# Moving one rest projection out of the last segment into the feed-forward network, with new load and copy orders and a new list of planner biases

## The chip, the cores and the metric

The kernel runs on one core of one Trainium2 chip. The metric is device time in microseconds (us), the median of several executions. A core has five instruction streams that run beside each other and meet at semaphores: TensorE (PE, with its weight loads listed as PEld), VectorE (DVE), ScalarE (ACT), GpSimd (POOL) and SyncE (SP). SP issues most DMAs; ACT issues a few at the start.

## The reference

What is computed is one transformer layer over 2048 tokens of width 640. The attention half is recurrent: the tokens come in 64 segments of 32, each segment puts 8 memory rows in front of its 32 tokens, attends within these 40 rows with 32 heads of 128, and hands the first 8 rows of its output to the next segment as memory.

```python
for s in range(n_seg):                       # 64 segments
    xs = x[:, s*32:(s+1)*32, :]              # of layernorm(x)
    h = concatenate([mem, xs], axis=1)       # 8 + 32 rows
    q, k, v = (einsum('btd,dhe->bhte', h, W) for W in (Wq, Wk, Wv))
    scores = where(mask, einsum('bhqe,bhke->bhqk', q, k) * scale, -1e9)
    o = einsum('bhqk,bhke->bhqe', softmax(scores), v)
    o = einsum('bhte,hed->btd', o, Wo)
    mem = o[:, :8, :]
    outs.append(o[:, 8:, :])
h = x + concatenate(outs)
hn = layernorm(h)
gate, up = hn @ W_gate, hn @ W_up            # width 1728
out = h + (gate * (gate > 0) * up) @ W_down
```

## The kernel before, in words

**Main rows and rest rows.** Of the 40 rows of a segment, 32 (8 of memory and the first 24 tokens) are the main rows, and the last 8 tokens are the rest rows. Nothing later in the recurrence needs the rest rows' output. So the queries, keys and values of the rest rows of four segments (a "quad") are computed together, in six parts (function `rest`: two query, two key and two value groups), and the output projection of the rest rows of eight segments together (`rest_o`, eight pieces of 16 matmuls, then a copy into `osr`, and `rest_out` stores it to DRAM). `oTr` keeps the rest rows' attention output until then. Five quads' rest parts are computed while the weights still load (`EARLY = 5`); the others are spread over the segments as filler for PE.

**A segment** (`segment`, called 64 times): queries, keys and values of the main rows (`groups`, line 1561), scores (lines 1860 and 1864), exponentials, sums, and the product with the values (1899, 1904), then the output projection in two halves: `wo_early` (1932) goes to a bank of its own and is kept as a high and a low part in `half`, `wo` (1951) goes to the bank BW, `wo_add` (1968) adds the two parts there. From BW the new memory rows are copied into the input of the next segment (1673) and transposed (1676), which the next segment's first matmul needs; BW is also evicted to `osb` and stored. `load_rs` brings the rest rows' queries, keys and values of the next segment from DRAM into `RS`. For the first segment they come straight from SBUF instead: POOL copies queries and keys (line 1596, the four "RS0" copies), and eight small DMAs on ACT's queue bring the values (line 1605).

**The feed-forward network** (`ffn`, four blocks of 512 tokens): 27 groups of five matmuls for gate and up (1729), the ReLU on ACT (1746), the product on DVE into `gT` (1748), and the projection down (1762, and 1539 for its last 128 columns). Its weights overwrite the attention weights: `Wg`, `Wu` and `Wl` go where Wq was, `Wd` and the second block's tokens `xn2T[1]` where Wk was. Three empty POOL instructions (named B0, B1, B2) wait for the last readers of Wq, Wk and Wv. The second halves of `Wg` and `Wu`, and `Wd` and `Wl`, also wait for `("osb", 1)`, that is for the last segment's eviction. `ln2` prepares 128 tokens of input (the last two are named tn2) with 20 PE transposes (1703).

**What sets the order.** Every instruction is described by `op` with what it reads and writes, a duration, and for a DMA a latency `lat` and a transfer time `xfer`. A list scheduler (`_Sched.schedule`) plays these through in simulated time and always takes the ready instruction of the highest level; the level is the length of the chain behind it plus entries of a dictionary `BIAS`, per name or per name and segment. `ENGINE` does the same for the choice between ACT and DVE. The result is one fixed order for each engine. In `op`, `x=` uses a buffer in sequence, and `beside=` reads it beside other readers: an instruction with `beside` waits for the last `x` user of that buffer, and if that is a DMA, for its landing.

Of the kernel before, what the change touches and what calls it, by code (L numbers as in the profile page):

```python
# [101 lines left out]
    "QK0mm@52": 27.88, "QK0mm@53": -4.68, "QK1mm@53": 4.98, "ln2l@62": 13.26, "sc1@62": -3.61,  # L102
    "ln2hd@62": 10.81, "Q1mm@62": -6.46, "Q0mm@64": 8.09, "QTx@64": -2.17, "QTx@63": -8.42, "exp1@62": -2.42,
    "mask0@63": 8.07, "sum0@64": -12.03, "QTx@51": -3.23, "oTev1@62": -0.16, "sum0@62": 1.43,
    "woadd@63": -14.73, "Q0mm@63": 5.22, "K1mm@64": -4.8, "ln1@64": -1.18, "hiev@64": -0.37, "loev@64": -6.44,
    "r0T@13": -7.71, "r0T@23": -0.83, "ln2s0@24": -1.25, "r0T@28": -0.32, "r1T@15": -7.85, "r0T@15": 39.2,
    "ln2s1@20": 18.36, "r1T@24": 6.73, "r0T@30": 7.0, "r0T@41": 9.76, "r0T@2": -4.21, "r0T@8": 4.31,
    "r1T@10": 8.26, "r1T@21": -1.66, "r0T@34": -44.8, "r1T@35": -14.61, "r0T@35": 5.08, "r0T@46": 7.34,
    "r1T@50": 20.94, "er1T@0": 6.64, "er0T@0": -26.24, "r1T@3": 22.75, "r1T@5": -2.15, "r1T@8": -22.29,
    "r0T@9": 20.78, "r1T@14": -3.91, "r0T@18": 3.15, "ln2a@24": 13.36, "r0T@25": 9.56, "r1T@36": 0.02,  # L110
    "r0T@39": 1.08, "r1T@40": 11.66, "r0T@44": -2.9, "r1T@45": 3.51, "r1T@47": 3.89, "r0T@49": -0.32,
    "r0T@51": 2.95, "r1T@52": 0.76, "r1T@55": -2.63, "r0T@55": -3.49, "r0T@56": 3.81, "r1T@57": 6.98,
    "ln2n@62": -3.77, "mask1@63": 0.92, "sum1@63": 7.18, "K0ev@62": -9.88, "mem1@63": -6.51, "loev@63": 2.39,
    "V1ev@63": 6.09, "K1ev@63": 0.32, "V0ev@64": 0.58, "rec1@64": -6.08, "K0Tev@64": -5.8, "K1ev@64": -10.81,
    "V1mm@64": -0.18, "oTev0@64": 2.09, "Q0Tev@64": -1.41, "wo1@64": 6.66, "Q0ev@64": 0.81, "sum1@64": -12.04,
    "mul0@64": -2.8, "K0ev@64": -11.69, "relu@65": 25.24, "tn2s0@65": -1.18, "Q1ev@64": -10.94,
    "tn2nd@65": -3.0, "hld@65": 17.53, "outdma@65": 9.49, "ordma@64": -2.27, "exp0@64": 8.26, "mask0@64": -8.5,
    "Q1mm@64": -7.79, "tn2go@65": -4.67, "tn2hd@65": 2.15, "V0mm@64": -4.09, "xnld@65": 3.31, "tn2x@65": 8.72,
    "tn2s1@65": 0.3, "ln0@64": 0.66, "pv0@64": 8.76, "tn2lx@65": -0.14, "tn2a@65": 5.97, "hadd@65": -8.82,
    "tn2lo@65": 18.63, "tn2Tev@65": 66.88, "gmul@65": 38.27, "mask1@64": -2.1, "ordma@61": 0.68,  # L120
    "K1mm@62": -2.64, "ln2a@32": 1.68, "mem1@54": 19.25, "ln2s0@20": 4.7, "ln2lx@32": 1.54, "ln2T@40": 0.7,
    "QTx@54": -1.51, "mask0@60": 19.52, "mask0@62": -1.74, "mask0@61": -3.7, "rec1@62": 4.5,
    "mask1@62": -25.63, "memcp0@61": -5.77, "ln2x@40": 4.41, "mask1@57": -2.39, "V1ev@57": -4.21,
    "rsdma@59": -7.2, "mask1@59": -16.78, "ln2s0@30": 8.32, "ln2lo@32": 7.27, "ln2l@32": 22.24,
    "ln2s1@54": -2.75, "wo1@54": -23.1, "mem1@56": -5.5, "mask0@57": 17.55, "ln2lx@20": 1.69, "ln2hd@24": -6.4,
    "ln2x@32": -1.4, "ln2l@24": 1.61, "ln2h@24": 2.68, "ln2s0@32": -11.95, "ln2h@32": 1.55, "ln2hd@32": 16.71,
    "rsdma@36": -0.43, "ln2a@38": -32.25, "QTx@31": 16.39, "ln2h@20": -1.42, "ln2s1@24": -5.03,
    "ln2lx@38": 0.61, "rsdma@8": 1.0, "ln2s0@38": 8.48, "ln2T@24": -19.85, "QTx@28": 0.22, "ln2a@30": -0.12,
    "rsdma@4": -14.78, "rsdma@29": 0.41, "rsdma@7": -13.97, "ln2n@24": -3.43, "rsdma@21": 4.61,
    "rsdma@26": 0.46, "ln0@44": -19.76, "ln2T@48": 7.82, "QTx@25": 0.35, "ln2Tev@32": -3.04, "QTx@36": 6.15,  # L130
    "ln2T@38": -9.4, "mask0@49": -23.75, "memcp0@50": -4.66, "mask0@51": 1.55, "QTx@3": 1.1, "QTx@8": 5.1,
    "oTev0@11": 9.98, "ln2n@20": -14.18, "ln2l@20": 0.52, "ln2a@22": 0.34, "QTx@6": -9.67, "mask1@14": -4.57,
    "rsdma@15": 0.65, "mask0@15": -5.34, "rsdma@16": 10.8, "mask1@18": 12.67, "ordma@21": -11.36,
    "ln2h@22": 4.04, "ln2go@22": 6.72, "mem1@22": -8.44, "mul1@32": 16.46, "mask1@32": -7.94, "mask0@32": 8.03,
    "QTx@35": -0.91, "QTx@41": -5.6, "rsdma@42": -28.29, "rsdma@44": -6.1, "QTx@45": 10.15, "ln2h@46": -4.12,
    "mask1@45": -34.49, "mask1@8": 0.75, "mask1@9": -9.21, "Q0ev@9": 4.52, "mask1@10": 20.02, "mul0@11": -6.33,
    "mask0@11": -0.34, "QTx@12": -5.38, "mask1@11": -6.32, "rsdma@12": 21.59, "mask1@13": -12.11,
    "QTx@17": 0.18, "QTx@20": -1.41, "ln2s1@22": -22.73, "rsdma@23": -3.62, "ln2Tev@24": 4.24,
    "rec0@25": 11.71, "mask1@25": -10.43, "mask1@26": -4.35, "mask0@26": 11.01, "rsdma@28": -9.74,
    "oTev1@27": -3.41, "ln2s1@30": 5.57, "rsdma@30": 2.9, "ln2go@30": 13.11, "mask0@29": -2.33,  # L140
    "mul0@32": -13.05, "osbev@32": -11.15, "rsdma@34": -7.0, "r0mm@34": 3.46, "mask1@36": -1.19,
    "mask0@36": -6.31, "ln2s1@38": -2.92, "ln1a@37": 5.12, "rvev@38": -7.09, "K0Tev@38": -3.05,
    "K1ev@38": 4.09, "ln0@38": 25.33, "mask1@40": -21.13, "ln1@39": -12.34, "ln2nd@40": 1.61, "oTr@40": 1.21,
    "V1mm@40": -23.61, "pv1@42": 15.48, "wo0@41": -12.36, "mask1@44": 2.73, "QTx@47": -7.4, "mask1@47": 0.39,
    "wo1@48": -6.53, "woadd@48": -0.94, "Q1Tev@48": -22.44, "rec0@49": 14.97, "K1ev@50": -22.66,
    "mask1@52": 2.07, "rsdma@56": 23.48, "mask1@56": -13.76, "mask0@55": 6.73, "mem@57": 3.55, "pv0@56": 37.91,
    "K0mm@57": -1.0, "K1mm@57": -7.64, "ln1@57": 0.04, "QTx@58": -0.49, "oTr@57": 1.27, "Q0Tev@57": -0.75,
    "mask0@58": 5.69, "ln1st@57": 22.78, "K0ev@57": -7.75, "QTx@59": -6.65, "mask1@58": -4.84,
    "memcp1@59": -23.71, "mask1@60": -4.13, "rsdma@60": -7.28, "mask0@3": 0.21, "rsdma@5": -0.43,
    "mask0@4": 0.63, "mask0@9": -1.77, "rsdma@11": 1.74, "mask0@12": -0.31, "K0ev@13": -8.19,  # L150
    "mask0@16": -1.48, "rec0@20": -12.18, "mul0@20": 8.24, "ln2s0@22": 4.2, "ln2hd@22": -8.09,
    "mask0@22": -6.66, "rec0@22": 5.09, "mask1@24": 14.94, "K1ev@24": 5.7, "mask0@25": 13.6, "mask1@27": 4.96,
    "mem@27": 1.4, "mask0@27": 2.3, "loev@27": -2.04, "ln1x@29": 6.46, "mask0@28": 4.98, "V0mm@28": -0.14,
    "Q0ev@28": 0.07, "mask0@30": 1.91, "mask0@33": 17.07, "exp0@33": -17.09, "Q0ev@34": 7.51, "mask0@34": 0.01,
    "mask1@34": 11.47, "rsdma@35": 15.6, "mask1@35": 11.79, "mask0@35": -48.34, "pv1@36": -13.73,
    "sum0@37": -34.01, "ln1st@37": -0.63, "rec1@37": -27.48, "ln2nd@38": 7.35, "wo1@37": -6.45,
    "mask0@38": -0.44, "ord@40": 3.35, "mask0@39": 0.2, "mask0@40": 70.66, "Q0ev@40": 12.0, "ln1a@41": -33.12,
    "mask0@41": -17.95, "mask1@41": -0.08, "mask0@43": -27.08, "rvev@42": 8.57, "mask0@42": -9.38,
    "woadd@42": -4.45, "mul1@42": 2.47, "mask1@42": -0.36, "memcp1@42": -21.72, "rec0@42": -5.61,
    "ln1@45": -4.83, "mask0@45": 13.85, "QTx@46": -1.55, "mul1@46": 0.02, "ln2go@46": -0.06, "ln1a@45": -8.84,  # L160
    "ln2Tev@46": -4.54, "loev@46": -3.2, "mask1@46": -7.16, "mask0@47": 3.07, "mask0@48": 16.0,
    "Q0ev@48": 8.46, "mask1@48": -3.59, "odma@48": -3.95, "oTev0@48": -1.77, "wo0@48": 4.31, "mem1@49": 5.25,
    "mask1@49": 2.88, "K0ev@49": 7.94, "mask1@50": 7.95, "mask0@52": 7.12, "mask0@53": 0.32, "mask1@53": 1.8,
    "mask1@54": 3.2, "ln2hd@54": -17.49, "mask0@54": 7.2, "odma@56": -23.33, "mask1@55": -21.92,
    "ln1@56": 4.16, "woadd@56": -0.17, "mem1@3": 0.36, "oTr@5": 0.37, "mask0@6": 20.33, "K1mm@8": -0.72,
    "mask0@8": -39.65, "ln1@10": 11.1, "sum1@10": -19.62, "mask0@10": -10.12, "mem@12": 2.29, "mask1@12": 0.3,
    "mask0@13": -2.1, "mask1@15": 5.83, "mask1@16": -0.88, "odma@16": 33.32, "rsdma@17": -4.35,
    "ln1n@17": -4.15, "memcp1@18": -7.07, "rsdma@18": -0.42, "K0mm@17": 28.43, "ro@17": 15.04,
# [1093 lines left out]
def build_kernel(nc, A_x, A_mem0, A_Wq, A_Wk, A_Wv, A_Wo, A_seg_len, B_x, B_W_gate, B_W_up,  # L1262
# [816 lines left out]
    for k in normed + list(range(NQ - 2, NQ)):  # L2079
        ln2(k)  # L2080
# [66 lines left out]
```

## Time and profile before

| | |
|---|---|
| median of 3 runs | 1050.86 us (1050.62 to 1051.02) |
| the profiled execution, its own time | 1052.89 us |
| its span, first to last instruction | 1051.2 us |
| PE busy | 993.4 us (95%) |
| DVE, ACT, POOL busy | 652.5, 488.1, 108.4 us |
| span 0 to 74 us (weights load) | PE busy 51.66 us |
| span 74 to 860 us (segments 2 to 64) | PE busy 756.28 us |
| span 896 to 1051.2 us (most of the feed-forward network) | PE busy 151.89 us of 155.20 |

The profiled execution is 1.69 us longer than its span and 2.03 us longer than the median of the runs. PE counts as busy while a matmul streams, whatever the clock; the granted clock is a column of its own in the table by stretches. In a row of the timeline the columns are start, length, engine, line, operation and tiles, then in brackets the idle time of the engine before it and what ended it. "issue" means that the engine waited for nothing that the profile shows.

### The profile page before, as it was taken

How to read it: one execution, taken by the hardware profiler on the slowest of the kernel's cores; microseconds unless marked ns; L12 is line 12 of the kernel's file. 1: busy time of each engine (PE TensorE's matmuls, PEld its weight loads, DVE VectorE, ACT ScalarE, POOL GpSimd, SP SyncE). 2: the span in 40 equal slices, each digit the busy share in tenths (PEclk: the TensorE clock that was granted, in tenths of full speed). 3: DMA queues.
4: the chain of work that ended last, by engine and by line, in shares of the span. 5: the costliest groups of instructions: out<-in, count | busy, mean ns of one | idle time of the engine just before them, and what ended most of it. 6: DMA issues, size and time to landing. Idle time of an engine off the chain costs nothing.

```text
span 1051.2 us, 53190 instructions
## 1 busy us (share of the span) xinstructions
PE 993.4 (95%) x24820; PEld 534.8 (51%) x23828; DVE 652.5 (62%) x1404; ACT 488.1 (46%) x1161; POOL 108.4 (10%) x262
## 2 busy tenths in 40 slices
PE   5699999999999999999999999999999989999998
PEld 2245555655565555655555555655555444444443
DVE  4457767677777767776777677667865642432233
ACT  2334555455556545555665455645554632121210
POOL 2301101011011101110101011011110010000000
PEclk9999999999999999999999999999999999999999
DMA  9991112121222112221222122212211237111101
GB/s 328 397 286 47 49 37 55 32 54 50 80 54 73 38 42 60 73 66 33 80 69 54 32 69 58 66 28 76 70 49 31 77 117 219 65 38 44 32 20 57
DMA packets 119212, 84.26 MB, mean 80 GB/s; under 512 B 71556, under 2 KB 115148, under 8 KB 118988
## 3 DMA queue, kind: packets, MB, share of 16 engines
q1 hardware_dynamic: 115628, 78.13, 24.9%
q8 instruction: 191, 3.13, 1.3%
q10 hardware_dynamic: 3360, 2.73, 0.8%
q14 instruction: 33, 0.27, 0.1%
HBM read 55.05 MB, written 25.69 MB: 77 GB/s over the span
## 4 chain that ended last, share of the span: by engine, by line
PE 86%; DVE 4%; ACT 2%; issue 2%; DMA 1%; ACTq 0%; POOL 0%; SPq 0%
PE ps L1561 45%; PE ps L1729 11%; PE ps L1932 7%; PE ps L1951 7%; PE ps L1762 5%; PE ps L1647 3%; PE ps L1899 2%; PE ps L1539 2%; PE ps L1874 1%; PE ps L1860 1%; DVE xT L1676 1%; DVE xm L1673 1%; DVE oT L1402 1%; DMA RS<-stg 1%; ACTq L1605 0%
## 5 line engine op out<-in xcount | busy, mean ns | idle before, releaser
L1401 ACT ACTIVATE tok<-ps 128x512 bf16<-128x512 f32 x241 | 142.2, 596 | 177.6 <-PE ps L1561 162.5
L1561 PE MATMUL ps<-Wk,xT 128*32 128x512 bf16 x2560 | 178.0, 380 | 14.2 <-DVE xT L1676 10.2
L1561 PE MATMUL ps<-Wq,xT 128*32 128x512 bf16 x2560 | 178.4, 379 | 6.1 <-DVE xT L1676 6.0
L1561 PE MATMUL ps<-Wv,xT 128*32 128x512 bf16 x2560 | 175.2, 380 | 0.2 <-DMA Wv<-in_A_Wv_dram 0.2
L1981 DVE STREAM_TRANSPOSE KT<-tok 128x512 bf16<-128x512 bf16 x128 | 89.6, 704 | 35.2 <-ACT tok L1401 33.7
L1981 DVE STREAM_TRANSPOSE QT<-tok 128x512 bf16<-128x512 bf16 x128 | 90.3, 706 | 32.8 <-ACT tok L1401 30.1
L1561 PEld LDWEIGHTS ps<-Wk,xT 128*32 128x32 bf16 x2560 | 67.1, 96 | 82.3 <-DVE xT L1676 20.9
L1561 PEld LDWEIGHTS ps<-Wq,xT 128*32 128x32 bf16 x2560 | 67.5, 96 | 72.2 <-DVE xT L1676 12.2
L1402 DVE CAST oT<-ps 128x320 bf16<-128x320 f32 x127 | 60.3, 488 | 54.7 <-PE ps L1904 51.8
L1932 PE MATMUL ps<-Wo,oT 128*32 128x320 bf16 x2048 | 90.9, 300 | 3.3 <-DVE oT L1402 3.2
L1951 PE MATMUL ps<-Wo,oT 128*32 128x160 bf16 x4096 | 86.2, 233 | 6.6 <-issue 4.9
L1746 ACT ACTIVATE g<-ps 128x512 bf16<-128x512 f32 (+1 forms) x56 | 33.4, 596 | 124.8 <-PE ps L1729 124.8
L1951 PEld LDWEIGHTS ps<-Wo,oT 128*32 128x32 bf16 x4096 | 74.3, 97 | 22.2 <-DVE oT L1402 9.5
L1748 DVE TENSOR_TENSOR gT<-g,ps 128x512 bf16<-128x512 bf16 (+1 forms) x56 | 37.5, 686 | 77.3 <-PE ps L1729 47.1
L1401 ACT ACTIVATE oT<-ps 128x320 bf16<-128x320 f32 x129 | 54.0, 435 | 54.9 <-PE ps L1904 53.2
L1561 PEld LDWEIGHTS ps<-Wv,xT 128*32 128x32 bf16 x2560 | 59.7, 96 | 38.0 <-ACT tok L1401 1.0
L1846 POOL COPY QT<-RS 128x256 bf16<-128x256 bf16 x64 | 25.8, 403 | 457.6 <-PE ps L1864 457.1
L1402 DVE CAST tok<-ps 128x512 bf16<-128x512 f32 x79 | 52.9, 670 | 24.8 <-PE ps L1561 24.5
L1869 ACT ACTIVATE E<-ps 128x224 bf16<-128x224 f32 x128 | 45.6, 356 | 43.0 <-PE ps L1864 42.2
L1729 PE MATMUL ps<-xn2T,Wg 128*128 128x512 bf16 x260 | 63.3, 379 | 0.3 <-DVE gT L1748 0.3
L1729 PE MATMUL ps<-xn2T,Wu 128*128 128x512 bf16 x260 | 63.3, 379 | 0.0
L1762 PE MATMUL ps<-Wd,gT 128*128 128x512 bf16 x224 | 61.7, 379 | 0.0
(93 smaller groups left out, 1444.6 us busy)
## 6 DMA issues: line engine op xcount, KB each, us to landing
RS<-scr_qk SPq DMA_DIRECT2D x63, 128.0 KB, 2.3
big<-in_A_x_dram SPq DMA_DIRECT2D x36, 160.0 KB, 2.8
scr_qk<-stg SPq DMA_DIRECT2D x44, 128.0 KB, 2.2
Wq<-in_A_Wq_dram SPq DMA_DIRECT2D x10, 512.0 KB, 7.3
Wk<-in_A_Wk_dram SPq DMA_DIRECT2D x10, 512.0 KB, 7.4
Wv<-in_A_Wv_dram SPq DMA_DIRECT2D x10, 512.0 KB, 8.1
Wo<-in_A_Wo_dram SPq DMA_DIRECT2D x8, 640.0 KB, 10.8
scr_v<-stg SPq DMA_DIRECT2D x32, 128.0 KB, 2.7
```

Of the source, the lines that this page charges most:

```text
L1401: return e.activation(dst, src, ACTF.Copy)
L1402: return e.tensor_copy(dst, src)
L1561: o = pe.matmul(out, lhs[c], rhs, start=(c == 0), stop=(c == DC - 1), skip_group_check=True)
L1647: o = pe.matmul(bank(bk)[p0:p0 + 32, 0:2 * SLICE], oTr[b][:, 16 * g + 4 * j + i, 32 * y:32 * y + 32], cols(h, 2 * a, 2 * a + 2), start=(h ...
L1729: o = pe.matmul(bank(bk)[:, 0:TB], lhs(c), xT[:, :, c * 128:(c + 1) * 128], start=(c == 0), stop=(c == DC - 1))
L1746: op("act", lambda a, t=t, lo=lo, hi=hi, bg=bg: a.activation(g1[t.at][lo:128, :], bank(bg)[0:hi, 0:TB], ACTF.Relu), r=["B2"], x=[bg, t], d ...
L1748: op("dve", lambda v, t=t, lo=lo, j=j, bu=bu: v.tensor_tensor(gT[lo:128, j, :], g1[t.at][lo:128, :], bank(bu)[lo:128, 0:TB], ALU.mult), r= ...
L1762: pe.matmul(bank(ba)[:, 0:512], lhs, Wd[:, j, 0:512], start=(j == 0), stop=(j == FC - 1), skip_group_check=True)
L1869: op("act", lambda a: a.activation(E[:, g, :, 0:56], sco(BS[g]), ACTF.Exp, scale=SCALE), r=["table"], w=[("E", g)], x=[BS[g]], dur=0.36, n ...
L1932: o = pe.matmul(bank(BA)[p0:p0 + 32, 0:2 * SLICE], oT[:, 4 * jj + i, XR:40], cols(h, 2 * b2, 2 * b2 + 2), start=(i == 0 and jj < 2), stop= ...
L1951: o = pe.matmul(bank(BW)[32 * j:32 * j + 32, 0:SLICE], oT[:, 16 + 4 * jj + i, XR:40], cols(h, j, j + 1), start=(i == 0 and jj == 0), stop= ...
L1981: op("dve", lambda v, tb=tb, dst=dst: v.transpose(dst, tok[tb.at][:, :].rearrange("p (h r) -> p h r", r=32)), w=[("QT" if p == 0 else "KT" ...
```

## The change

It does five things.

1. The last eight segments' `rest_o` no longer stands in segment 64. It is called after `ffn(0)`, in four parts of two pieces each, and part k waits for the product `gT[2k+1]` of the first block. The last two `ln2` and blocks 1 to 3 follow in the program's text; the scheduler decides the order of instructions as before.
2. The second block's tokens (`xnld` of block 1) wait for the load of `Wl`, the last of the feed-forward weights. Before, they waited for B1 alone.
3. The four RS0 copies stand ahead of the stores of the same buffers and no longer wait for these stores to land. The stores read the buffer beside them.
4. Three figures of the planner change: 1.09 for 0.8 us (the POOL copy `ord`), 3.4 for 2.0 us (latency of the eight value DMAs), and 1.0 us more for the first weight load.
5. `BIAS` is another list (2142 entries with another value, 591 new, 481 gone, spread over all segments), and so is `ENGINE` (71 changed, 159 new, 128 gone).

```diff
@@ rest / spread
-                    stg[t1.at]...(u i k)...), x=[t1, t2], dur=0.8, name=early + "ord")
-            op("act" if early else "sp", lambda e: e.dma_start(
-                scr_qk[q, 2 * p + g, :, :], stg[t2.at][:, :]), w=[("scr_qk", q, p, g)], x=[t2], dur=0.4,
-               lat=2.2, chan=("rqe", 12) if early else ("rq", 4), name=early + "rdma", xfer=0.35)
+                    stg[t1.at]...(u i k)...), x=[t1, t2], dur=1.09, name=early + "ord")
             if q == 0:
                 k = 2 * p + g
                 op("pool", lambda e: e.tensor_copy(RS[0][:, 128 * k:128 * k + 128], stg[t2.at][:, 0:128]),
                    w=[("RS0", k)], beside=[t2], dur=0.31, name="RS0")
+            op("act" if early else "sp", lambda e: e.dma_start(
+                scr_qk[q, 2 * p + g, :, :], stg[t2.at][:, :]), w=[("scr_qk", q, p, g)], beside=[t2], dur=0.4,
+               lat=2.2, chan=("rqe", 12) if early else ("rq", 4), name=early + "rdma", xfer=0.35)
@@ rest / values
-                       w=[("RSv0", g, j)], beside=[tb], dur=0.7, lat=2.0, chan=("rv0", 8), name="ldrs", xfer=0.05, desc=2)
+                       w=[("RSv0", g, j)], beside=[tb], dur=0.7, lat=3.4, chan=("rv0", 8), name="ldrs", xfer=0.05, desc=2)
@@ ffn
-            op("sp", ... scr_n[4 * b + u]), r=[("scr_n", 4 * b + u)] + (["B1"] if home else []),
+            op("sp", ... scr_n[4 * b + u]), r=[("scr_n", 4 * b + u)] + (["B1"] if home else []) + ["Wl"] * (b == 1),
@@ load_w
-           xfer=xfer + (1.4 if nload[0] == 2 else 0.0), desc=desc)
+           xfer=xfer + {1: 1.0, 2: 1.4}.get(nload[0], 0.0), desc=desc)
@@ segment
-        if s == NSEG - 1:
-            rest_o(s // 8, B("rest"), (0, 8))
-            rest_out(s // 8)
@@ behind the loads of the feed-forward weights
+    ffn(0)
+    bk = B("rest")
+    for k in range(4):
+        rest_o(NSEG // 8 - 1, bk, (2 * k, 2 * k + 2), [("gT", 2 * k + 1)])
+    rest_out(NSEG // 8 - 1)
     for k in normed + list(range(NQ - 2, NQ)):
         ln2(k)
-    for b in range(NBLK):
+    for b in range(1, NBLK):
         ffn(b)
```

## The prediction

> **What bounds the kernel now.** I read the page first, then the chain of work that ended last, then three places where it leaves PE's matmuls: the end of the segments, the start, the gaps between segments.
>
> ```profile
> PE 993.4 (95%) x24820; PEld 534.8 (51%) x23828; DVE 652.5 (62%) x1404; ACT 488.1 (46%) x1161; POOL 108.4 (10%) x262
> ...
> PE 86%; DVE 4%; ACT 2%; issue 2%; DMA 1%; ACTq 0%; POOL 0%; SPq 0%
> ```
>
> PE bounds it: 95% busy and 86% of the chain. The change takes no matmul away, so it can only win time in which PE idles or runs at a lower clock, and lose by adding such time.
>
> The end of the segments, PE's timeline, then the table by stretches (length, busy times by engine, then granted clock, DMA share, GB/s):
>
> ```profile
> 859.00 0.74 PE L1951 MATMUL ps<-Wo,oT 128*32 128x160 bf16 x32 [0.66 <-DVE oT L1402]
> 859.55 0.86 PE L1647 MATMUL ps<-Wo,oTr 128*32 128x320 bf16 x18
> 862.53 5.54 PE L1647 MATMUL ps<-Wo,oTr 128*32 128x320 bf16 x110 [2.13 <-issue]
> ...
> 868.70 2.33 PE L1729 MATMUL ps<-xn2T,Wg 128*128 128x512 bf16 x10
> ```
>
> ```profile
> 862.00:864.00 2.00, 1.47 (x24) 0.95 (x28) 0.00 (x0) 0.00 (x0) 0.00 (x0) 0.58 0.44 167
> 864.00:866.00 2.00, 2.00 (x40) 1.22 (x33) 0.00 (x0) 0.00 (x0) 0.00 (x0) 0.56 0.05 15
> ```
>
> The 128 matmuls to be moved (L1647) stand ahead of the second half of the last segment's projection. After 18 of them PE idles 2.13 us for "issue", and then runs at a clock of 0.56 until 866. The page lists 191 packets in its instruction queue q8; 24820 + 23828 PE instructions over 191 are 255 each: a packet is a page of PE's instructions. The trace has such packets at 851.27 and 860.09 us, 8.8 us apart where four or five is usual, while the feed-forward weights load. I read the 2.13 us as a late page.
>
> SP's timeline over the same time:
>
> ```profile
> 852.64 1.75 SPq L1722 DMA_DIRECT2D xn2T<-scr_n  x4
> 854.43 0.43 SPq L2069 DMA_DIRECT2D Wg<-in_B_W_gate_dram  x1
> 854.90 0.53 SPq L2069 DMA_DIRECT2D Wu<-in_B_W_up_dram  x1
> 869.15 0.37 SPq L2069 DMA_DIRECT2D Wg<-in_B_W_gate_dram  x1
> ```
>
> The first weights land 7.4 and 9.9 us after issue, at 861.8 and 864.8. The second halves go out at 869.15 only, behind the last eviction.
>
> **The tail, step by step.** Matmuls of L1647 at full clock come at 1.09 us per 32 elsewhere in the chain, so 128 are 4.36 us wherever they stand. From 859.73 to 868.76 there are 9.03 us: 4.36 for them, about 0.8 for the rest of L1951 and the adding, and 3.8 of loss (2.13 idle, 1.7 at the low clock: 5.47 us for the 110 against 3.75).
>
> After the change PE goes from 859.73 straight to the adding and is ready for the feed-forward network at 860.5. SP need not issue four token loads first: Wg goes out when Wq's last reader (853.7) is through, at 854.0 to 854.4, and 640 KB less stand before it. The second halves, alone on the queues, landed 5.1 us (960 KB) and 7.8 us (both) after the first issue; scaled to 1120 KB that is 6.0 and 9.1, hence Wg at 860.2 and Wu at 863.3. Two gate groups (2 x 1.08) bridge from 860.5 to 862.7, so about 0.5 us of waiting is left. The 3.8 us of loss go, if no page is late.
>
> What is added: four visits of L1647 between wide matmuls. The nearest rows are the transposes inside the network:
>
> ```profile
> 898.09 1.24 PE L1729 MATMUL ps<-xn2T,Wg 128*128 128x512 bf16 x5
> 899.26 0.46 PE L1703 MATMUL ps<-ident,big 128*32 128x128 bf16 x20
> 899.65 1.25 PE L1729 MATMUL ps<-xn2T,Wu 128*128 128x512 bf16 x5
> ```
>
> Five wide matmuls take 1.08 us start to start, here 1.17 and (to the next transposes, at 900.84) 1.19: 0.10 us for a change of tile shape, eight changes 0.8 us (bounds 0, if the visits go side by side, and 1.2). Tail: 3.8 - 0.5 - 0.8 = **2.5 us won**. Bounds: 3.3 won; 0.8 lost, if idle time and low clock return.
>
> The rest of the tail costs nothing. The second weight halves go out some 8 us earlier. Block 1's tokens go behind Wl: landed at about 884 before (877.89 + 6.5), plus 1.75 us of issue and 2.6 to land is 888.5, and block 1's first group runs at about 902 (25 of the 160 gate and up matmuls before 907.8 are its own). SP waits in order, and behind these four loads stand the `osr` stores, the last two `ln2` and the loads of scr_h; a few us there are covered, since the last two `ln2` feed only block 3, after 990. That cover gone, it would be 1 us for 1 us.
>
> **The start.** PE's longest wait from 46 to 74 us (total, times, longest), and POOL's timeline:
>
> ```profile
> PE ps L1860 <- POOL QT L1846: 2.5, 1, 2.5
> ```
>
> ```profile
> 46.38 0.29 POOL L1596 COPY RS<-stg 128x128 bf16<-128x128 bf16 x1 [0.24 <-DMA scr_qk<-stg]
> ...
> 48.98 0.29 POOL L1596 COPY RS<-stg 128x128 bf16<-128x128 bf16 x1
> 49.45 0.40 POOL L1846 COPY QT<-RS 128x256 bf16<-128x256 bf16 x1 [0.17 <-POOLq L1837]
> ```
>
> The first scores wait for L1846, which waits for the RS0 copies, which wait for stores to land and stand behind further copies. Ahead of the stores the last RS0 copy can run at about 43.3, where its source is done. The idle 2.52 us at 47.4 then need not be; nor the low clock behind it (0.5 from 49.96 to 56.79; 48 wide matmuls there cost 2.6 us more). But PE lacks weights: the last four loads of Wv land at 48.2, 50.2, 51.8 and 53.4 (issue plus 8.8 to 9.2), so much of that idle time only moves. The end of this stage is floored too: the last Wo load goes out at 58.1 and lands 10.6 later, at 68.7; a quarter of L1951 (0.28), the adding (0.3), copy and transpose (about 1.3) let segment 2 start at 70.6 against 73.84. So 0 to 3.2 us; I take **1.3 won**, below the middle, because the eight value DMAs still issue one by one behind Wv (57.10 to 62.87, the last lands at 67.92).
>
> **The segments.** From segment 2 to 64 PE idles 28.6 us in gaps of over 0.15 us; the largest causes from 74 to 856:
>
> ```profile
> PE ps L1561 <- DVE xT L1676: 16.2, 35, 0.8
> PE ps L1951 <- issue: 4.9, 11, 1.0
> ```
>
> The new biases redo the order in every segment. Bounds: all new gaps and all old ones are the same kind, so half of the 16.2 us lost or won. Nothing in the profile says which; I take **0**, with 3 us either way.
>
> **The sum.** 1052.89 - 2.5 - 1.3 = 1049.1 for the profiled execution. It stands 2.03 above the median, so **1047.0 us**, 0.37% faster.
>
> **Rivals.**
> - *The tail wait stays* (0.25). A late page needs the weights' traffic and some 250 quick PE instructions; both remain up to 860.5, and then the network issues 10 per 1.08 us, which any page survives. In my count the page ends 36 instructions after 859.73, still inside L1951; some 40 instructions fewer ahead of it and it falls into the network. If it stays, so does the low clock: 0.8 lost, 1.3 won, 1050.4. The Trainium skill ("TensorE: Matmul & The Clock Gate", Part 1) lets the clock halve only after an idle window of about 3.4 us; by that rule the same wait would leave the clock full and this rival would give 1048.7. The trace speaks against it: 0.56 after 2.13 us.
> - *The segments win more* (0.15): a quarter of their idle time less 3 us already in the range, so 4 us beyond the sum: 1043.
> - *Slower* (0.10): late pages inside the segments. Eleven waits of L1951 for "issue" cost 4.9 us now, 0.45 each. A tighter order sends the narrow matmuls in denser runs; if their number doubles, the tail's wait stays and the start gives nothing, it is 1050.9 + 4.9 + 0.8 = 1056.6. With these two it decides from three more such waits. Against it: at 0.4 us idle per segment there is little room to be denser.
> - *It does not do what it says*: the scheduler could put the four parts together after block 0's last gate group. That saves six shape changes, 0.6 us, and stays within the forecast.
>
> Of the page wait itself the Trainium skill ("Runtime: NRT & Kernel Launch", Instruction fetch mechanics) says that PE holds 2048 instructions and that a refill is mostly hidden; by it no page could be late here and the tail's 2.5 us would be safe. The 2.13 us beside the packet at 860.09 say otherwise.
>
> **Chances.** Forecast 0.50, within about 2 us of 1047.0. What a measurement of this kernel can tell from no change is about 0.2%, 2.1 us: faster means below 1048.8. Of the forecast 0.42 lies there, of the stayed wait 0.05, of the third case all 0.15: faster 0.62; same 0.28; slower 0.10. The range is 1043.0 to 1051.0: it leaves out the slower rival and a little of the segments' win.
>
> **What would show it.** Right: no L1647 before the first L1729 of the network, that one at 860 to 862, no "issue" of over 1 us and a clock of 1.0 from 858 to 870; L1846's first run at 44 to 47; segment 2 (its first L1561 on xT) at 71 to 73. Wrong: an "issue" wait before the network, or a wait of the network for Wu of over 1 us; PE's idle time in the segments up by over 3 us; block 1 waiting for its tokens.

## The result: 0.56% slower

The changed kernel takes 1055.83 us in the median (1053.47 to 1058.48) beside 1050.63 us (1048.27 to 1054.4) for the kernel before in the same comparison: a ratio of 1.0056, 95% interval 1.0038 to 1.0074. The prediction, 1047.0 us within 1043.0 to 1051.0, was wrong, in sign too. Below, each experiment stands against runs of the kernel before taken beside it. Single executions of one kernel spread over up to 10.6 us, so a verdict rests on ratios of medians, and the place of a gain or loss on the stages of one profiled execution, which lies between 3.2 us below the median of its kernel and 2.8 above: a difference of a few us between whole spans, or in the long stretch of segments 2 to 60, can be the choice of execution.

The profiled execution after takes 1058.48 us, the slowest of its seven; its span is 1056.4 us, 5.2 more than before. The page of the kernel after, its engines and its chain:

```profile
PE 997.4 (94%) x24804; PEld 535.4 (51%) x23828; DVE 668.1 (63%) x1429; ACT 475.3 (45%) x1136; POOL 109.4 (10%) x262
...
PE 86%; DVE 4%; DMA 2%; issue 2%; ACT 1%; SPq 0%; ACTq 0%; DVEq 0%
```

PE still bounds it, and a DMA has come into the chain. I cut the span where DVE starts to copy the new memory rows (L1673 before, L1702 after), once per segment:

| us | start, to segment 2 | segments 2 to 60 | 61 | 62, 63 | 64 to the end | span |
|---|---|---|---|---|---|---|
| before | 72.85 | 739.22 | 12.67 | 23.81 | 202.62 | 1051.2 |
| after | 78.36 | 734.54 | 15.14 | 23.51 | 204.87 | 1056.4 |
| difference | +5.51 | -4.68 | +2.47 | -0.30 | +2.25 | +5.2 |

Three places lose and one wins.

**The start.** PE's timeline after, then three of the waits from 46 to 74 us (total, times, longest):

```profile
63.78 1.47 PE L1590 MATMUL ps<-Wv,xr 128*32 128x512 bf16 x24
70.07 0.32 PE L1928 MATMUL ps<-E,Vm 32*128 32x40 bf16 x16 [4.82 <-DVE stg L1431]
```

```profile
ACT stg L1430 <- DMA scr_qk<-stg: 7.0, 2, 4.7
DVE stg L1431 <- DMA scr_qk<-stg: 6.2, 2, 4.2
...
PE ps L1889 <- POOL QT L1875: 2.6, 1, 2.6
```

PE idles 4.82 us for copies into `stg`, and both copying engines wait for stores of scr_qk to land. Behind the wait the granted clock is low, the last column but two here:

```profile
69.20:76.00 6.80, 5.67 (x120) 3.23 (x124) 3.23 (x6) 2.19 (x5) 0.00 (x0) 0.50 0.76 171
```

The line of L1889 above is the wait that was to go; before it was 2.5. ACT's timeline over the same time, and the time from issue to landing in the table of DMAs from 56 to 72 us:

```profile
56.07 6.20 ACTq L1634 DMA_DIRECT2D RS<-stg  x8
62.31 0.95 ACTq L1624 DMA_DIRECT2D scr_qk<-stg  x2
...
70.05 0.60 ACT L1430 ACTIVATE stg<-ps 128x512 bf16<-128x512 f32 x1 [4.74 <-DMA scr_qk<-stg]
```

```profile
scr_qk<-stg ACTq DMA_DIRECT2D x2, 128.0 KB, 7.0
```

Two early stores stand on ACT's queue behind the eight value DMAs, go out at 62.31 and need 7.0 us beside the last loads of Wo. The planner has given two of the six value copies behind them the same two staging buffers (numbers 4 and 5; in the kernel before, the three behind the stores took 9 to 11), reckoning with 2.95 us for such a store. POOL's timeline shows why the wait for QT stayed:

```profile
43.21 5.57 POOL L1617 COPY stg<-stg 128x512 bf16<-128x512 bf16 x5 [0.86 <-DMA scr_qk<-stg]
48.95 0.40 POOL L1875 COPY QT<-RS 128x256 bf16<-128x256 bf16 x1 [0.17 <-POOLq L1866]
```

The last RS0 copy ended at 42.35, sooner than predicted. But the copy of the queries, L1875 (L1846 before), stands behind five `ord` copies in the new order, and runs at 48.95 where it ran at 49.45.

**The end of the segments.** PE's timeline after, SP's, and one stretch (length, busy times by engine, then the clock):

```profile
861.90 1.01 PE L1980 MATMUL ps<-Wo,oT 128*32 128x160 bf16 x47 [0.66 <-DVE oT L1431]
865.43 0.83 PE L1980 MATMUL ps<-Wo,oT 128*32 128x160 bf16 x17 [2.53 <-issue]
...
866.46 4.45 PE L1758 MATMUL ps<-xn2T,Wg 128*128 128x512 bf16 x10
870.70 2.62 PE L1758 MATMUL ps<-xn2T,Wu 128*128 128x512 bf16 x10
```

```profile
857.02 0.38 SPq L2095 DMA_DIRECT2D Wg<-in_B_W_gate_dram  x1
857.44 0.53 SPq L2095 DMA_DIRECT2D Wu<-in_B_W_up_dram  x1
```

```profile
866.00:868.00 2.00, 2.00 (x20) 0.65 (x6) 0.32 (x1) 0.00 (x0) 0.00 (x0) 0.50 0.10 15
```

The rest projection is gone from here, yet the wait for "issue" is there, 2.53 us now, in the next instructions that came: the second half of the last segment's projection. The half clock behind it now covers the network's first ten matmuls, 4.24 us instead of 2.16.

**The segments.** From 74 to 812 us the two largest waits of PE, before and then after:

```profile
PE ps L1561 <- DVE xT L1676: 14.1, 31, 0.8
PE ps L1951 <- issue: 4.9, 11, 1.0
```

```profile
PE ps L1590 <- DVE xT L1705: 13.1, 30, 0.7
PE ps L1980 <- issue: 3.6, 9, 0.8
```

Segment 61 gives half of the gain back; PE's timeline, then SP's:

```profile
822.37 0.28 PE L1928 MATMUL ps<-E,Vm 32*128 32x40 bf16 x16 [1.38 <-DMA RS<-scr_v]
```

```profile
814.19 0.56 SPq L1637 DMA_DIRECT2D scr_v<-stg  x1
...
817.87 1.14 SPq L1657 DMA_DIRECT2D RS<-scr_v  x2
```

The last quad's values are stored at 814.19 and read back from 817.87 on; PE waits 1.38 us for them, and a stretch of half clock (3.41 us from 823.5) follows.

### The profile page after: what moved, and what is told of

Read it like the earlier page. It is cut to its first block, busy times and chain, and to the rows that moved or that the text cites. A ratio compares the mean times of both kernels' runs of the same rounds, so it can differ in the third digit from the quotient of the medians.

```text
span 1056.4 us, 53183 instructions
## 1 busy us (share of the span) xinstructions
PE 997.4 (94%) x24804; PEld 535.4 (51%) x23828; DVE 668.1 (63%) x1429; ACT 475.3 (45%) x1136; POOL 109.4 (10%) x262
## 4 chain that ended last, share of the span: by engine, by line
PE 86%; DVE 4%; DMA 2%; issue 2%; ACT 1%; SPq 0%; ACTq 0%; DVEq 0%
PE ps L1590 44%; PE ps L1758 11%; PE ps L1961 7%; PE ps L1980 7%; PE ps L1791 4%; PE ps L1676 3%; PE ps L1928 3%; PE ps L1568 2%; PE ps L1903 1%; DMA scr_qk<-stg 1%; PE ps L1889 1%; DVE xT L1705 1%; DVE xm L1702 1%; PE ps L1933 0%; DVE oT L1431 0%
## 5 line engine op out<-in xcount | busy, mean ns | idle before, releaser
L1430 ACT ACTIVATE tok<-ps 128x512 bf16<-128x512 f32 x230 | 135.9, 596 | 182.7 <-PE ps L1590 178.1
L1590 PE MATMUL ps<-Wk,xT 128*32 128x512 bf16 x2560 | 180.9, 380 | 11.7 <-DVE xT L1705 10.4
L1431 DVE CAST oT<-ps 128x320 bf16<-128x320 f32 x136 | 64.7, 489 | 60.5 <-PE ps L1933 59.7
L1961 PE MATMUL ps<-Wo,oT 128*32 128x320 bf16 x2048 | 93.1, 305 | 2.5 <-DVE oT L1431 2.5
L1980 PEld LDWEIGHTS ps<-Wo,oT 128*32 128x32 bf16 x4096 | 75.2, 98 | 23.4 <-DVE oT L1431 9.8
L1431 DVE CAST tok<-ps 128x512 bf16<-128x512 f32 x90 | 60.6, 675 | 25.9 <-PE ps L1590 25.1
L1430 ACT ACTIVATE oT<-ps 128x320 bf16<-128x320 f32 x120 | 50.9, 436 | 50.3 <-PE ps L1933 48.2
L1875 POOL COPY QT<-RS 128x256 bf16<-128x256 bf16 x64 | 26.3, 410 | 447.6 <-PE ps L1893 447.1
L1758 PE MATMUL ps<-xn2T,Wg 128*128 128x512 bf16 x260 | 66.5, 389 | 0.1
L1961 PEld LDWEIGHTS ps<-Wo,oT 128*32 128x32 bf16 x2048 | 48.8, 97 | 24.3 <-DVE oT L1431 8.7
```

Of the source, the lines that this page charges most:

```text
L1430: return e.activation(dst, src, ACTF.Copy)
L1431: return e.tensor_copy(dst, src)
L1590: o = pe.matmul(out, lhs[c], rhs, start=(c == 0), stop=(c == DC - 1), skip_group_check=True)
L1758: o = pe.matmul(bank(bk)[:, 0:TB], lhs(c), xT[:, :, c * 128:(c + 1) * 128], start=(c == 0), stop=(c == DC - 1))
L1961: o = pe.matmul(bank(BA)[p0:p0 + 32, 0:2 * SLICE], oT[:, 4 * jj + i, XR:40], cols(h, 2 * b2, 2 * b2 + 2), start=(i == 0 and jj < 2), stop= ...
L1980: o = pe.matmul(bank(BW)[32 * j:32 * j + 32, 0:SLICE], oT[:, 16 + 4 * jj + i, XR:40], cols(h, j, j + 1), start=(i == 0 and jj == 0), stop= ...
```

## The experiments

My theory after the result: the start loses to the staging buffers alone, and the tail to a page of PE's instructions whose packet comes late because it is asked for after the feed-forward weights have been issued. Rivals: the new structure or the new order as such costs the time; the moved projection costs it; the tail's wait is a matter of how quick the instructions are, wherever a page ends. In the table, "to the network" runs from the copy of segment 64 to the first wide matmul, and the page wait is the "issue" wait of PE around 850 to 875 us. Medians and ratios stand against the kernel before in the same comparison (1050.6 to 1053.4 there); two medians from different comparisons carry that difference too.

| kernel | start | 2 to 60 | 61 | 64 to the end | to the network | page wait | median | ratio (95%) |
|---|---|---|---|---|---|---|---|---|
| before | 72.85 | 739.22 | 12.67 | 202.62 | 20.16 | 2.13 | 1050.63 | 1 |
| after | 78.36 | 734.54 | 15.14 | 204.87 | 14.90 | 2.53 | 1055.83 | 1.0056 (1.0038 to 1.0074) |
| s1_buffers | 72.18 | 736.19 | 14.88 | 204.90 | 15.20 | 2.83 | 1050.66 | 0.9990 (0.9974 to 1.0007) |
| s2_scores_early | 70.32 | 734.36 | 13.09 | 203.39 | 14.90 | 2.52 | 1049.66 | 0.9966 (0.9949 to 0.9982) |
| t1_rest_back | 78.75 | 735.27 | 13.50 | 203.42 | 20.32 | 2.30 | 1055.40 | 1.0034 (1.0019 to 1.0049) |
| b1_tail | 71.79 | 741.65 | 12.76 | 204.04 | 14.91 | 2.46 | 1054.05 | 1.0019 (1.0002 to 1.0036) |
| p1_shift | 76.10 | 735.34 | 13.90 | 201.38 | 11.70 | none | 1054.67 | 1.0022 (1.0008 to 1.0036) |
| p3_shift_page | 76.92 | 737.26 | 15.18 | 205.02 | 15.21 | 2.84 | 1059.13 | 1.0058 (1.0039 to 1.0077) |
| b3_before_shift | 72.44 | 742.34 | 14.32 | 201.43 | 18.97 | 2.49 | 1055.17 | 1.0014 (0.9997 to 1.0032) |
| p2_shift_rest_back | 76.82 | 737.00 | 15.22 | 200.77 | 17.53 | 1.19 | 1055.41 | 1.0020 (1.0004 to 1.0035) |
| h1_both | 72.45 | 737.28 | 13.87 | 200.68 | 11.70 | none | 1050.21 | 0.9980 (0.9960 to 1.0000) |
| h2_both_small | 72.23 | 738.46 | 14.30 | 201.80 | 11.70 | none | 1050.84 | 0.9981 (0.9964 to 0.9998) |
| h3_all | 72.60 | 740.00 | 14.02 | 200.88 | 11.70 | none | 1050.87 | 0.9975 (0.9959 to 0.9992) |
| s3_early_rest_back | 70.21 | 736.30 | 13.06 | 201.90 | 18.62 | 2.29 | 1048.66 | 0.9968 (0.9948 to 0.9988) |

No kernel leaves work out. The three p kernels, b3_before_shift and the three h kernels add matmuls of zeros.

**s1_buffers** changes only which staging buffers the early value copies take; the order on every engine is that of the kernel after.

```diff
-            tb = _Slot("stg", range(nst))
+            tb = _Slot("stg", range(nst - 1, -1, -1) if q < EARLY else range(nst))
```

> The changed kernel with one edit: the values of the first five quads of rest rows look for a staging buffer from the highest number down instead of from the lowest up. The order of every engine stays the same; only buffer numbers change, so that no value eviction waits for a buffer whose store (issued at 62.31 us behind the eight value DMAs) lands only at 70 us. Theory A (the start lost its time to this buffer wait): PE's idle time of 4.8 us before the first product with the values goes, the low clock from 69.2 to 76.0 us goes with it, the new memory rows of segment 2 come at 72 to 74 us instead of 78.4, and the kernel is 4 to 6 us faster than the changed one (about 1050). Rival B (the start is bound by the value DMAs behind the Wo load anyway): the wait only turns into a wait for DMA RS<-stg, segment 2 starts no earlier than 76.5 us, under 2 us come back.

Its timeline of PE has the matmuls that waited 4.82 us:

```profile
65.81 0.27 PE L1928 MATMUL ps<-E,Vm 32*128 32x40 bf16 x16 [0.54 <-DVE stg L1431]
```

The start falls from 78.36 to 72.18, the median by 5.2 us and the ratio from 1.0056 to 0.9990: a loss of the size of the whole one goes with the buffer numbers. What is left against the kernel before, 2.3 us lost in the tail beside 3.0 won in segments 2 to 60, cancels out.

**s2_scores_early** adds a bias to s1_buffers, so that POOL takes the copy of segment 1's queries ahead of the last four `ord` copies.

```diff
+BIAS.update({"QTx@1": 600.0, "RS0": 600.0})
```

> The changed kernel with the buffers of the start cured, and the copy of the rest rows' queries for segment 1 (L1875) put ahead of the last five copies of the staging buffers on POOL by two large biases. Tests the start's step of the prediction: PE's wait for L1875 (2.9 us) goes. Theory A (it is no loss, PE only waits for the last Wv loads instead, until 53): segment 2 within 0.7 us of 72.2, the time within 1 us of the buffers alone. Rival B (as the prediction had it): 1.3 us or more faster, segment 2 at 71 us or sooner.

POOL's timeline, then PE's wait from 46 to 74 us:

```profile
46.30 0.40 POOL L1878 COPY QT<-RS 128x256 bf16<-128x256 bf16 x1
```

```profile
PE ps L1892 <- POOL QT L1878: 0.4, 1, 0.4
```

The copy runs 2.65 us earlier than in the kernel after, the wait of the scores falls from 2.9 us in s1_buffers to 0.4, and segment 2 starts at 70.32, 1.86 sooner. The prediction had reckoned with a floor of 70.6 there, set by the last load of Wo; that load goes out at 55.84 here and lands at 67.85, where it went out at 58.12 before and landed at 69.08 (the prediction's 68.7 was misread). The median moves from 1050.66 to 1049.66; the ratios' intervals overlap, so a gain of the whole kernel over s1_buffers is not shown, and the profiled execution here is the fastest of its twelve.

**t1_rest_back** undoes part 1 in the kernel after, **b1_tail** puts parts 1 and 2 alone into the kernel before (its diff is that of parts 1 and 2 above). The diff of t1_rest_back, shortened:

```diff
-    ffn(0)
-    bk = B("rest")
-    for k in range(4): rest_o(..., (2 * k, 2 * k + 2), [("gT", 2 * k + 1)])
-    rest_out(NSEG // 8 - 1)
...
+        if s == NSEG - 1:
+            rest_o(s // 8, B("rest"), (0, 8)); rest_out(s // 8)
```

> The changed kernel with the last eight segments' rest projection back in segment 64 (part 1 of the change undone, part 2 kept); the order up to segment 64 is the same. Theory A (moving it won nothing because the late page and the low clock stay, and added about 0.8 us of changes of tile shape): within 1.5 us of the changed kernel, either way; the wait for issue of 2 to 2.5 us stands in the tail again. Rival B (the move itself costs what was lost in the tail): 2 us or more faster than the changed kernel. Rival C (the move does win what was forecast): 2.5 us slower.

> The kernel before with parts 1 and 2 of the change alone (rest projection in the first block, second block's tokens behind the last weights), with its own planner lists; its order up to segment 64 is the same. Theory A (the tail's two parts alone win nothing): 0 to 1.5 us slower than before, a wait for issue of about 2 us just ahead of the first feed-forward matmuls, segment 2 at 73 us as before. Rival B (the tail's parts explain the loss): 3 us or more slower. Rival C (as forecast): 2.5 us faster.

Undoing part 1 takes 0.4 us off the median, with intervals that overlap, and 1.45 off the tail; parts 1 and 2 alone make the kernel before 0.19% slower. All four kernels, with or without the move, have one late page of 2.1 to 2.5 us behind the weights' issue.

**p1_shift** and **p3_shift_page** add 80 and 128 matmuls with as many weight loads in PE's idle first 9 us. They sum zeros that nothing reads. In p1_shift (45 and 35 of them) every later page of PE's instructions ends 160 instructions sooner in the work; in p3_shift_page (72 and 56) 256 sooner, which is a whole page, so that each end falls where one fell. The diff of p1_shift, shortened:

```diff
+    def extra(pe, n):
+        for i in range(n): pe.matmul(ps[...32 columns...], ident[...], E[...32 columns...])
...
+            if b == 7: extra(pe, 45)
...
+            if r == 0: extra(pe, 35)
```

> The changed kernel with 80 narrow matmuls and their 80 weight loads more on PE in its idle time of the first 9 us, which shifts every later page of PE's instructions by 160; nothing else in the order changes. They add zeros to a part of a bank that nothing reads. Theory A (the 2.5 us wait for issue ahead of the feed-forward network is a page of PE instructions that is fetched late because it is asked for after the weights began to load): the request falls ahead of the weights, the wait goes (under 0.5 us) and with it the low clock in the network's first 5 us; 3 to 5 us less from segment 64 to the end. Rival B (the wait has another cause, such as the weights' landing or a semaphore): it stays at 2 us or more at the same place. Other waits for issue in the segments (3.6 us in all) will fall elsewhere, by 2 us either way.

> The control for the shift: the kernel after with 128 matmuls and their 128 weight loads (of zeros, into a sum that nothing reads) in PE's idle first 9 us, which is one whole page of 256 instructions, so that every later page ends at the same instruction of the work as in the kernel after. By my theory only where a page ends counts: the tail's wait comes back at the same place, inside L1980 with some 47 of its 64 matmuls done, 2 to 2.8 us long, and from the copy of segment 64 to the network it is 14.9 again, the tail 203.4 to 204.9, with or without a low clock. Rival: that the shift by 160 helped through something else (the extra work itself, another rhythm of the transfers); then the wait is gone here too, 11.7 to the network and a tail of 200.7 to 201.8.

PE's timeline of p1_shift, then of p3_shift_page:

```profile
860.56 2.33 PE L1766 MATMUL ps<-xn2T,Wg 128*128 128x512 bf16 x10
864.78 2.33 PE L1766 MATMUL ps<-xn2T,Wu 128*128 128x512 bf16 x10 [1.88 <-DMA Wu<-in_B_W_up_dram]
```

```profile
867.40 0.83 PE L1990 MATMUL ps<-Wo,oT 128*32 128x160 bf16 x17 [2.84 <-issue]
```

With the shift the wait is gone, the first ten matmuls of the network run at full clock, and it is 11.70 us to the network instead of 14.90. With a whole page the wait is back between the same two matmuls, 47 of 64 done. So it is where pages end that counts, and not the extra work. The count of instructions says the same of every such wait: in the fourteen profiles PE waits 123 times for "issue" by more than 0.3 us, and each time the number of matmuls, weight loads and semaphore instructions that PE has behind it is 193 more than a multiple of 256. So pages end there. The packets of the queue q8 fit it; each row is the packet that PE waits for, or would wait for:

```
kernel             packet starts   PE instructions     Wg, Wu issued     wait
                                   into the page
before             860.09          254                 854.43, 854.90    2.13
after              862.83          256                 857.02, 857.44    2.53
p3_shift_page      864.79          256                 858.67, 859.10    2.84
b3_before_shift    866.72          256                 859.18, 860.42    2.49
s3_early_rest_back 854.48          253                 848.67, 849.10    2.29
p1_shift           854.42           62                 854.32, 854.75    none
```

Elsewhere three quarters of the packets start within the first 100 instructions of a page, for the page after it; these five come some 200 instructions late, with PE at or near a standstill. In eight of the nine kernels with a wait of over 2 us the packet starts 5.7 to 6.1 us after Wg is issued (7.5 in b3_before_shift), and PE goes on 6.7 to 7.0 us after it entered the page before. The planner counts pages too, in both kernels (`PAGE = 256`), but gives each one the same 3.85 us. That the weights' packets hold these up is read from the times of issue; no run took the weights away.

**b3_before_shift** is the same shift of 160 in the kernel before.

> The kernel before with nothing but the 80 extra matmuls and their loads in PE's idle first 9 us. If the tail's wait is a page of instructions asked for behind the feed-forward weights, the kernel before is mended by the same shift: the page that is asked for at 856.8 there is asked for at about 852, ahead of the first weights at 854.4, the 2.13 us wait at 862.5 and the low clock behind it go, and from the copy of segment 64 to the first wide matmul it is 17 instead of 20.2; tail 199.5, span 1048, ratio 0.997. The moved projection would then be worth nothing that the shift does not give alone. Rival: in the kernel before the wait belongs to the 128 matmuls of L1647 in one run, wherever the page falls (quick instructions use a page up faster than it is filled): then a wait of 1 to 2 us returns at another instruction of L1647 and the tail stays at 201.5 to 203.

```profile
869.28 2.35 PE L1655 MATMUL ps<-Wo,oTr 128*32 128x320 bf16 x62 [2.49 <-issue]
```

My theory's forecast failed. The first page came in time, but the next one, 48 matmuls further on, ended inside the rest projection too (66 of 128 done, 18 before) and was late in its turn: 128 quick matmuls use a page up while the weights still load. This is the rival's case, and the one thing that the moved projection is good for: in p1_shift and the h kernels that next page falls among the network's matmuls and nothing waits for it.

**p2_shift_rest_back** is the kernel after with the shift and with part 1 undone; **h1_both** is s1_buffers with the shift; **h2_both_small** is h1_both with first weight pieces of four column blocks instead of half the columns (`FH = 4 * 128`).

> The changed kernel with the rest projection back in segment 64 and the pages shifted by 160 instructions. Tells what the move is worth when the page falls well. Theory A (some 450 quick PE instructions run under the weights' traffic when the rest projection stands there, so that one page request always falls into it): a wait for issue of 1.5 us or more comes back, in or near L1676, the stretch from segment 64 to the end is 203 us or more against 201.4 with the move, 2 us slower. Rival B (the shift alone cures it): no such wait, 200 to 201 us, the move is worth nothing.

> The changed kernel with both cures: staging buffers of the early values from the highest number down, and the 160 narrow PE instructions in the idle start that shift the pages. The order stays that of the changed kernel. Theory A (the loss was the buffer wait of the start and the late page of the tail, and the new lists do win in the segments): segment 2 at 72 us, 735 us from there to segment 61 against 739 before, 201.4 us from segment 64 to the end, so 1046 to 1048.5, 3 to 5 us faster than before and 2 to 4 us faster than with the buffers alone. Rival B (the two gains do not add up, since an earlier start only meets later waits): 1050 or more.

> The kernel with both cures, and the first pieces of the gate and up weights cut from seven column blocks of 128 to four (the second pieces grow from six to nine). The wait for Wu (1.9 us with the page shifted) is a matter of its 1120 KB behind those of Wg; 640 KB each should land at 861 or sooner. Theory A: that wait falls under 0.4 us, the second pieces (issued at 861) land in time, 1 to 2 us faster than with both cures alone. Rival B: the second pieces land late and PE waits for them at the fifth column block, by 1 us or more; no gain or a loss.

PE's timeline of p2_shift_rest_back, then of h2_both_small:

```profile
866.99 2.47 PE L1684 MATMUL ps<-Wo,oTr 128*32 128x320 bf16 x65 [1.19 <-issue]
```

```profile
872.43 1.25 PE L1766 MATMUL ps<-xn2T,Wu 128*128 128x512 bf16 x5 [1.88 <-DMA Wu<-in_B_W_up_dram]
```

With the shift the tail is 200.77 with the projection back and 201.38 with it moved: what the move saves at the page it pays to Wu and to the changes of shape. The tail that was expected of p2_shift_rest_back, 203 or more, did not come; its rival's 200 to 201 did, though a wait of 1.19 us is left. Smaller first pieces only move the wait for Wu to the fifth column block (they also change the order there: four visits of the moved projection, not three). The forecast for h1_both, 1046 to 1048.5, missed. Against s1_buffers it wins 4.2 us in the tail and 3.8 in the span of the profiled execution, but only 0.1% in the ratios (0.9980 beside 0.9990, with intervals that overlap). Most of the 3.8 is the choice of execution: that of s1_buffers is the slowest of its twelve, 2.77 above the median, and that of h1_both lies 0.52 below its own. Where the runs lose what the tail wins stays open.

**h3_all** (s2_scores_early with the shift) and **s3_early_rest_back** (s2_scores_early with part 1 undone) ask whether the gains add.

> All three mends together on the kernel after: the early value evictions take the free staging buffers, the rotated queries of segment 1 (L1875) and the RS0 copies stand ahead of the ord copies on POOL, and 80 matmuls with their weight loads (of zeros, into a sum that nothing reads) in PE's idle first 9 us move every later page of instructions by 160. By my theory the causes are apart from each other and add: segment 2 starts at 70.3 to 70.6 as with the early queries, segments 2 to 61 take 734 to 737, from the copy of segment 64 to the network 11.7 and to the end 201 to 201.8, no 'issue' wait of over 1 us from 850 to 875; span about 1043.5 and a median some 5 us below that of before (ratio 0.995). Rival: the sum is held by something that every version shares (the low clock in windows of 3.41 us that fall anywhere, or the wait for Wu behind Wg), so that each mend wins alone but the sum is no better than the early queries alone: ratio 0.997 or above.

> The version with the free staging buffers and the early queries of segment 1, but with the last rest projection back in segment 64 (part 1 of the change undone, the rest of the change left). If part 1 is worth nothing on this chip, as undoing it from the kernel after showed: start 70.3, segments 2 to 61 734 to 737, tail 203 to 203.5 (20.3 to the network, with a late page inside L1676), median within 1 us of 1049.7, ratio 0.996 to 0.998. Rival: part 1 wins its 2.5 us once the start's loss no longer hides it; then this version is 2 to 3 us slower than the one with the early queries, ratio 0.999 or above, and its tail is longer than 205.

PE's timeline of h3_all:

```profile
70.05 0.39 PE L1601 MATMUL ps<-Wk,xr 128*32 128x512 bf16 x1 [1.48 <-issue]
```

The sum did not come: h3_all has the good tail, 200.88, but the start has this new "issue" wait of 1.48 us, and seven such waits of over 0.6 us stand in its segments where s2_scores_early has one: the shift moves all pages, not only the one in the tail. Its ratio, 0.9975, is no better than that of the early queries alone. Part 1 undone there costs nothing: 0.9968 beside 0.9966. These two are the best versions, 0.3% faster than the kernel before. In both the wait for scr_v in segment 61 is gone; by what was not tried.

## Why the prediction was wrong, point by point

- **"The start: 1.3 won" failed; it lost 5.51.** The mechanism was right (with the buffers free, s2_scores_early starts segment 2 by 1.9 us sooner for it, 2.5 sooner than the kernel before), but I took it that the new order would use it, and in that order the queries' copy stayed behind `ord`. And a step was missing: which buffers the copies take, and which stores must have landed for that. I counted what the stores no longer hold up in POOL, not what they hold up through a buffer that is used again. s1_buffers settles it.
- **"Tail: 2.5 won" failed; it lost 2.25.** The named rival, "the tail wait stays", came true with its mechanism, a page that ends inside the second half of the last projection. Its 0.8 lost was too small: the wait is 0.4 longer, and low clock covers 6.8 us where 3.4 was. The prediction had counted where the page ends, 36 instructions after 859.73, which is behind 50 of the 64 matmuls; it came behind 47, and in b1_tail behind 50. The step that failed is the "if no page is late": with the page counted into the projection and the weights issued before it, the late page should have been the forecast and not a rival at 0.25.
- **Wu.** The 0.5 us of waiting are 1.2 to 1.9 where they can be seen (p1_shift, h1_both, h3_all): Wu lands 10.4 us after the first issue in p1_shift, 9.1 were scaled. With that and 0.6 for shapes, 3.8 leaves 1.3 to 2.0; the tails of these three are 1.2 to 1.9 shorter than before, not 2.5.
- **Shapes held** in the price of one change: five wide matmuls ahead of the moved projection take 1.17 us from start to start where 1.08 is usual, and 64 of its matmuls take 2.29 to the next wide one where 2.18 would do. But the scheduler put two of the four parts together, so there are three visits and six changes, some 0.6 us and not 0.8. Right, too, was the cover of block 1's tokens: issued at 885.41, and PE has no wait for them.
- **The segments, "0 within 3 us"**: 4.68 won less 2.47 in segment 61 and plus 0.30 makes 2.5 won. The new lists win over many segments: segments 2 to 60 take 734.4 to 738.5 us in ten of the eleven kernels with them (740.0 in h3_all), and 739.2 to 742.3 in the three with the old ones. The rival of 4 us more was nearer for segments 2 to 60 than my zero.
- **The rival "slower"** gave 1056.6, close to what came, by luck; its mechanism did not come: "issue" waits inside the segments fell from 4.9 to 3.6.
- **The page sentence**: the Trainium skill ("Runtime: NRT & Kernel Launch", Instruction fetch mechanics) has the refill mostly hidden; nine of the fourteen kernels here wait 2.1 to 2.8 us for one page.

## What to carry to other kernels

When a planner hands out buffers again, look for the DMA that still reads them, and give it the time from issue to landing that the trace shows in that stage (7.0 us here beside a bulk load, 1.9 in the median of the later ones), not one figure for all. A wait for "issue" belongs to a place in the instruction stream: moving work away hands it to what comes next. Count where pages end, ask which of them are due behind a large transfer, and give those the time that a late one took (6.7 to 7.0 us here, where the planner has 3.85).

## What the runs showed of the hardware

Low clock comes in stretches of 3.41 us on a grid that runs on through the span: in the kernel after, those at 823.5 and 864.5 lie 221 and 233 such steps behind the one at 69.2. Over the fourteen profiled executions, all 23 windows of the grid at full clock with PE busy for less than 0.42 of them were followed by one at half clock, and none with more than 0.53; of 17 between, 5 were (the first 17 and the last 8 us of each span are left aside). By this the same wait costs differently: 2.53 us in the kernel after fall mostly into one window (busy 0.35, half clock behind it), 2.49 us in b3_before_shift are split by the grid (busy 0.50, clock 1.0 behind it). The Trainium skill ("TensorE: Matmul & The Clock Gate", Part 1) has an idle window of about 3.4 us; the length agrees, that it must be idle throughout does not.
